# Causal scores on four 64 by 64 tiles of TensorE, with the halves of the keys exchanged in odd pairs of heads

## The chip, the core and the metric

The kernel runs on one core of a Trainium2 chip. A core has five engines with an instruction queue each: TensorE (PE, matrix products; PEld is its loading of weights), VectorE (DVE), ScalarE (ACT), GpSimd (POOL) and SyncE (SP, which here only issues DMAs). The metric is the device time of one execution in microseconds (us). The kernel before took 475.58 us (median of three runs, 474.87 to 476.09).

## What is computed

Two blocks follow each other, all in float32. The first is gated linear attention, for 4 batches, 8 heads, 768 positions and a head size of 48:

```
state = alpha[t][:, None] * state + outer(k[t], v[t])     # 48 x 48 per head
y[t]  = q[t] @ state
```

The heads' outputs are laid side by side to x with 384 columns. The second block is a two-layer perceptron with a residual:

```
xn  = (x - mean) / sqrt(var + 1e-6) * g_ln
out = x + max(xn @ w_ch1, 0) @ w_ch2                      # 384 -> 1536 -> 384
```

## The kernel before, in words

**Chunks.** The 768 positions are cut into 6 chunks of 128, so there are 24 attention blocks (chunk c, batch b), written a to x in the order string: a to d are chunk 0, e to h chunk 1, i to x chunks 2 to 5. Inside a block the recurrence becomes matrix products. The logarithms of alpha are summed along the chunk by a product with a triangle of ones (`lps`, L228); q is multiplied by the exponential of that sum and k by that of its negative (`qk`, L235 and L237); both are transposed per pair of heads (`tps`, L251) and copied to `qkT` (L255, L257). The two heads of a pair lie in rows 0 to 47 and 64 to 111.

**Scores (L264).** For each of four pairs and each of the two heads one matmul makes the full 128 keys by 128 queries, `aps[i][:, p]`. Keys are the stationary operand with 128 columns, queries the moving one with 128 columns, and the contraction runs over 48 rows. Head i goes to the PSUM buffer `aps[i]`. An fp32 matmul shows up in the trace as two passes, each a weight load and a matmul, so a block is 16 passes.

**Mask (L268).** One masked copy per head, `copy_predicated` on DVE, takes the scores with key not after query out of PSUM to `at` in SBUF. `at` was set to zero once, and the masked places are never written, so they stay zero. There are two `at`, used in turn.

**Weighted sum (L281, L286).** `yps` collects the state's part (from chunk 1 on) and the product of `at` with v, per pair, head and half of the queries. ACT copies it to `x` (L290), which lives till the perceptron adds it to its output. `sps` (L297) is the new part of the state, DVE adds it to `st` (L302), POOL multiplies `st` by the chunk's gate (L307). x is then normalized (L311 to L318), transposed (`xps`, L325) and copied to `xT` (L327).

**Perceptron.** Chunk 0 is computed plainly (`hidden`, L337, and `project`, L349). Chunks 1 to 5 use combinations of blocks with fewer products: 30 `hps` steps (L510) and 14 `ops` steps (L404) per chunk, whose sums run on DVE and POOL and partly on ACT.

**Buffers.** PSUM has three buffers with tag `a` (shared by `lps`, `tps` and `aps`), three with tag `m` (`hps`, `ops`) and two with tag `s` (`yps`, `sps`, `xps`). `x` has 9 buffers in SBUF. q, k, v and alpha have one raw buffer per batch and input; v of chunk c + 1 is loaded when the state of chunk c has been updated.

**Order.** Each part is a Python generator that yields between its steps. The string `ORDER` is a list of turns: each letter lets one generator take its next step (a to x the attention blocks, A to L the 12 pieces of weights, M the perceptron, S the combined weights, X and N the combined activations, R the relus). The order of instructions on each engine is that of the turns; semaphores make an engine wait where a result or a buffer isn't ready. A wait on TensorE holds everything behind it on TensorE.

```
    with tc.manual_schedule():
        for turn in ORDER:
            next(turns[turn], None)
```

Of the kernel before, what the change touches and what calls it, by code (L numbers as in the profile page):

```python
# [9 lines left out]
FP32 = mybir.dt.float32  # L10
INT32 = mybir.dt.int32
# [10 lines left out]


ORDER = (
    "ababdaacbaabccaabacdacbaabadcbbbdcdAabbbdaBcCccdabAeddbcbdcffcdfeegacfcbagdhfbde"
    "adbceBeegAdhfBCfdeabdfefcAheiBeafdeagjgbecfebcfcgeegfdefdgcghhihfdcgdegCCigMhMgD"
    "DhMjEMEjFMhiDkhfMgfighFheMFFfMMIMEIhIDMgEjhMGhMgjMhgfMGiHMMGGkMMMMHeiJMkMlHJMigM"
    "IMLJilHljMejKKjiLKeLjMhhfjSigSMhMlSMglSlhgiffMKkMhMhSSSMSSSMXiXkikXSXiimjMXXXSSM"
    "MXkMMSkjMMXkMkMMSMMjMmMMjXkmMSlmiMSMMiMkMMXkMjMMMlMlmRMmMMMokSjlMlMnlMnMljnkMMMR"
    "MjnMMMMSMMmMnMMmnRMMRRMoRSkiMlpklniMkpnjmMMRMmMRpkMRMNMMNmMlMiRkmMMiNMMnloMpRMSM"  # L30
    "njNMMkplMoRMMMkMMNmjNMMlMMNNmonnMljomqMMlqMMlnXMMXMXmXnXXMXqMMMXmmXMMooMMMMpMpMn"
    "MMXMMoMoMMMrMoXMnRqoRmoMpMMrpMMMMMMpMMpRnproMMmMMmqMMMrMMMqqMsMMnMnMpJqrRnqsMorM"
    "tMMMMmqMooRppMpotsRMMtRMtMrMRqMRNMoMNMRNMMrMpRMoNsMqMspqpMoMtMMRMMMNMNMMNMMMoMpn"
    "MpNsrrnMtrpqvrquXrXXrXMquXqXsMXsrMXrMqMMXMXuMMMMrMrMLMsMtXMMstMMMtqMsstMMMMMqvRR"
    "MMvMsuMsMtuMMRMMMrMMuwMMMMRMMMvwMvqMttqMMMruRMMRMMsMMRMMMMRMssRtwtsvutxvMRNsvMNN"
    "tMvNsRtRMMMvMtMMuusMMtMMwuuMrMMwwxNxMxvrtNNMMMNMMMtxsMMMuXMXXXMvMvuuXxXXMXvXuMMM"
    "MwwXwMMxMMxMXMMMMMMuvMMxMMuMMwRxMMMwwRMvMwMMMRxuxwxwwMuxMRxvMwMMMxxMMMMMRMMvMMuM"
    "RMMMvMMMxMMRuMRMMRMMNMMMNRMMNMMvMMNMMMwwMMvwMxxRNwRMMNMNNMMMMwxMMvxMXXXXXXMMMMXX"
    "XMMMMMMMMMXMMMMMMMMXMMMMMRRMMMMMMMMMMMMMRMMRMMMMMMMMMMRRMMMRMMRMMMMMMRMNMMMNRNMM"
    "MMNMMMMMMMRMNRMNMMNMMMMNMMMMMMMM"  # L40
)


# [1 line left out]
def kernel(  # L45
# [8 lines left out]
    w_ch2: bass.AP,  # L54
    out: bass.AP,
):

# [22 lines left out]
    nc = tc.nc  # L82

    B, S, H, D = q.shape
    DM = H * D
    DF = w_ch1.shape[1]
    P = 128
    NCB = S // P
    NP = H // 2
# [6 lines left out]
    cpool = ctx.enter_context(tc.tile_pool(name="const", bufs=1))  # L96
    raw = ctx.enter_context(tc.tile_pool(name="raw", bufs=B))
    stage = ctx.enter_context(tc.tile_pool(name="stage", bufs=STAGED))
    work = ctx.enter_context(tc.tile_pool(name="work", bufs=2))
# [5 lines left out]

    r = np.arange(P)
    upto = (r[None, :] >= r[:, None]).astype(np.float32)
    const_np = np.concatenate([upto, np.eye(P, dtype=np.float32)], 1)

    raws = {}  # L110

    def load(c, b, names="akqv"):
        for n, src in (("a", alpha), ("k", k), ("q", q), ("v", v)):
            if n not in names:
                continue
            t = raw.tile([P, H, D], FP32, name=f"r{n}", tag=f"r{n}",
                         bufs=B)
            nc.sync.dma_start(t, src[b, c * P:(c + 1) * P])
            raws[n, c, b] = t

    consts = cpool.tile([P, 2 * P], FP32, name="consts")
    nc.scalar.dma_start(consts, nc.inline_tensor(const_np, name="consts").ap())
    tri, ident = consts[:, :P], consts[:, P:]
    mask = tri.bitcast(INT32)
    for names in ("a", "kq", "v"):
        for b in range(B):
            load(0, b, names)
# [82 lines left out]
    ats = [cpool.tile([P, 2, NP, P], FP32, name=f"at{i}") for i in range(2)]  # L210
# [6 lines left out]
    x_of, xT_of, hT_of = ({} for _ in range(3))  # L217
# [3 lines left out]
    def attention(c, b):  # L221
# [21 lines left out]
        n = c * B + b + (B if c < 2 else B // 2)  # L243
        if c < 2 or 3 * B <= n < NCB * B:
            load(*divmod(n, B), "akq")
        yield
        qkT = work.tile([R, 2, NP, P], FP32, name="qkT", tag="qkT", bufs=2)
# [11 lines left out]
        at = ats[b % len(ats)]  # L259
        aps = [ps.tile([P, NP, P], FP32, name=f"aps{i}", tag="a", bufs=3) for i in range(2)]  # L260
        for p in range(NP):
            for i in range(2):
                rows = slice(64 * i, 64 * i + D)
                nc.tensor.matmul(aps[i][:, p], qkT[rows, 1, p], qkT[rows, 0, p],  # L264
                                 start=True, stop=True)
        yield
        for i in range(2):
            nc.vector.copy_predicated(out=at[:, i], data=aps[i],  # L268
                                      mask=mask.unsqueeze(1).broadcast_to([P, NP, P]))
        yield  # L270
        if c + 1 < NCB:
            with nc.allow_non_contiguous_dma(reason="one row to columns"):
                nc.sync.dma_start(gate, row.rearrange("o a c -> c (o a)"))
        yield
        vt = raws.pop(("v", c, b))
        yps = ps.tile([P, NP, 2, D], FP32, name="yps", tag="s")
        sides = [slice(64 * s, 64 * s + 64) for s in range(2)]
        for p in range(NP):
            if c > 0:
                for s in sides:  # L280
                    nc.tensor.matmul(yps[s, p].rearrange("p a b -> p (a b)"), qkT[:, 0, p, s],  # L281
                                     sts[b][:R, p].rearrange("p a b -> p (a b)"),
                                     start=True, stop=False)
            for i in range(2):
                for s in sides:
                    nc.tensor.matmul(yps[s, p, i], at[:, i, p, s], vt[:, 2 * p + i],  # L286
                                     start=(c == 0), stop=(c == 0 or i == 1))
        yield
        x_of[c, b] = x = work.tile([P, DM], FP32, name="x", tag="x", bufs=9)
        nc.scalar.copy(out=x, in_=yps.rearrange("p a b d -> p (a b d)"))  # L290
        yield
        if c + 1 < NCB:
# [11 lines left out]
        if c + 1 < NCB:  # L304
            load(c + 1, b, "v")
            st = sts[b].rearrange("p a b d -> p a (b d)")
            nc.gpsimd.tensor_mul(st, st, gate.unsqueeze(2).broadcast_to([P, NP, 2 * D]))  # L307
# [280 lines left out]
    def sums():  # L588
# [4 lines left out]
        yield from combine_weights()  # L593

    turns = {chr(ord("a") + n): attention(n // B, n % B) for n in range(NCB * B)}
    turns |= {chr(ord("A") + i): take_weights(i) for i in range(len(pieces))}
    turns |= {"M": mlp(), "S": sums(), "R": relus(),
# [35 lines left out]
```

## Time and profile before

| what | us |
|---|---|
| median of three runs | 475.58 |
| the profiled execution, first to last instruction | 471.8 |
| TensorE busy | 459.0 |
| DVE busy | 327.1 |
| POOL busy | 203.8 |
| ACT busy | 152.0 |
| masked copies, 48 of 724 ns | 32.2 |

Busy time of TensorE counts any time in which at least one matmul is under way. Matmuls are pipelined, and on different parts of the array several run at once, so the length of a group is read from the start of its first instruction to the start of what follows. In the lists of waits a line says which engine and line waited for which, then the total in us, how often, and the longest.

The same page in 40 slices of 11.8 us shows where TensorE and DVE are busy (in tenths):

```profile
PE   5989999999999999999999999999999999999997
DVE  4899997768456985567768378685656576675742
DMA  8988365203112102030211320120010000000000
```

### The profile page before, as it was taken

Reading aid. Unit: us, or ns where it says so; the run is one execution under the profiler, and the core shown is the slowest. Engines: PE = TensorE matmul, PEld = TensorE weight load, DVE = VectorE, ACT = ScalarE, POOL = GpSimd, SP = SyncE. Lnnn points to the kernel's source line nnn. Section 1 sums busy time; section 2 is a strip of 40 time slices with the busy share of each in tenths; the row PEclk is TensorE's granted clock in tenths of the full one; section 3 lists DMA queues with packets and bytes.
Section 4 is the critical chain, followed back from the end, with each engine's and each line's share of the span. In section 5 each row is a group of like instructions: output and inputs, shape, how many; then the busy total and the mean of one; then the engine's idle time right before and its main releaser. Section 6 shows DMA issues by size and latency. Waiting matters only on the chain.

```text
span 471.8 us, 9234 instructions
## 1 busy us (share of the span) xinstructions
PE 459.0 (97%) x3712; PEld 388.5 (82%) x3712; DVE 327.1 (69%) x571; ACT 152.0 (32%) x325; POOL 203.8 (43%) x203
## 2 busy tenths in 40 slices
PE   5989999999999999999999999999999999999997
PEld 3758654566788899988899998899998899987996
DVE  4899997768456985567768378685656576675742
ACT  5676533421132631114341133351203331123300
POOL 5034010049779873127553116573214281145611
PEclk9999999999999999999999999999999999999999
DMA  8988365203112102030211320120010000000000
GB/s 267 334 234 265 78 192 173 83 23 113 52 36 67 35 18 84 8 114 18 86 35 35 100 71 17 35 85 1 33 36 1 1 1 17 18 33 2 0 35 33
DMA packets 32498, 33.84 MB, mean 72 GB/s; under 512 B 13108, under 2 KB 28596, under 8 KB 32456
## 3 DMA queue, kind: packets, MB, share of 16 engines
q1 hardware_dynamic: 31912, 33.12, 22.8%
q8 instruction: 29, 0.48, 0.4%
q10 hardware_dynamic: 544, 0.13, 0.1%
q14 instruction: 13, 0.11, 0.1%
HBM read 28.49 MB, written 4.76 MB: 70 GB/s over the span
## 4 chain that ended last, share of the span: by engine, by line
PE 90%; DMA 4%; DVE 2%; POOL 2%; ACT 2%; SPq 0%; issue 0%; POOLq 0%; DVEq 0%
PE ops L404 29%; PE hps L510 26%; PE hps L337 7%; PE ops L349 7%; PE aps L264 5%; PE yps L286 4%; PE yps L281 4%; PE tps L251 3%; PE lps L228 2%; PE sps L297 2%; PE xps L325 2%; DMA rk<-in_k_dram 2%; DMA ws<-in_moe_w_ch_dram 1%; DMA ra<-in_alpha_dram 1%; DVE w L163 1%; ACT ws L169 0%
## 5 line engine op out<-in xcount | busy, mean ns | idle before, releaser
L307 POOL TENSOR_TENSOR st<-st,gate 128x384 f32<-128x384 f32 x20 | 20.6, 1034 | 76.7 <-issue 30.6
L510 PE MATMUL hps<-sum,w 128*128 128x256 f32 x200 | 51.7, 381 | 0.0
L404 PE MATMUL ops<-w,hT 128*128 128x192 f32 x240 | 42.5, 327 | 0.0
L404 PE MATMUL ops<-w,sum 128*128 128x192 f32 x240 | 42.4, 326 | 0.0
L404 PE MATMUL ops<-ws,hT 128*128 128x192 f32 x240 | 42.3, 326 | 0.0
L562 ACT ACTIVATE hT<-hT 128x512 f32<-128x512 f32 x60 | 36.6, 632 | 16.5 <-POOL hT L548 6.6
L510 PEld LDWEIGHTS hps<-sum,w 128*128 128x128 f32 x200 | 37.1, 190 | 5.2
L404 PEld LDWEIGHTS ops<-w,hT 128*128 128x128 f32 x240 | 39.3, 190 | 0.7
L404 PEld LDWEIGHTS ops<-w,sum 128*128 128x128 f32 x240 | 39.3, 190 | 0.3
L404 PEld LDWEIGHTS ops<-ws,hT 128*128 128x128 f32 x240 | 39.3, 190 | 0.0
L268 DVE COPY_PREDICATED at<-consts,aps 128x512 f32<-128x512 int32 x48 | 32.2, 724 | 10.2 <-PE aps L264 9.9
L286 PE MATMUL yps<-rv,at 128*64 128x48 f32 x768 | 36.4, 219 | 0.0
L422 POOL TENSOR_TENSOR ob<-u,x 128x192 f32<-128x192 f32 x10 | 6.9, 686 | 67.6 <-issue 42.8
L235 POOL TENSOR_TENSOR qk<-rk,ek 128x384 f32<-128x384 f32 x24 | 26.7, 1113 | 19.5 <-ACT ek L232 19.5
L286 PEld LDWEIGHTS yps<-rv,at 128*64 128x64 f32 x768 | 33.0, 137 | 1.3 <-issue 0.7
L529 POOL TENSOR_TENSOR hT<-hT,u 128x512 f32<-128x512 f32 x10 | 12.8, 1284 | 48.6 <-DVE u L528 48.5
L337 PE MATMUL hps<-xT,w 128*128 128x512 f32 x72 | 32.6, 598 | 0.0
L349 PE MATMUL ops<-w,hT 128*128 128x384 f32 x96 | 32.3, 488 | 0.0
L510 PE MATMUL hps<-xT,w 128*128 128x256 f32 x120 | 31.2, 383 | 0.0
L251 PE MATMUL tps<-consts,qk 128*112 128x128 f32 x192 | 29.2, 281 | 1.5 <-DVE at L268 1.0
L264 PE MATMUL aps<-qkT 48*128 48x128 f32 x384 | 28.6, 285 | 1.5 <-DVE at L268 0.8
L251 PEld LDWEIGHTS tps<-consts,qk 128*112 128x112 f32 x192 | 22.8, 137 | 8.8 <-issue 4.1
(127 smaller groups left out, 956.2 us busy)
## 6 DMA issues: line engine op xcount, KB each, us to landing
ws<-in_moe_w_ch_dram SPq DMA_DIRECT2D x12, 768.0 KB
ra<-in_alpha_dram SPq DMA_DIRECT2D x24, 192.0 KB
rk<-in_k_dram SPq DMA_DIRECT2D x24, 192.0 KB
rq<-in_q_dram SPq DMA_DIRECT2D x24, 192.0 KB
rv<-in_v_dram SPq DMA_DIRECT2D x24, 192.0 KB
out_dram<-ob SPq DMA_DIRECT2D x24, 192.0 KB
row<-eq SPq DMA_DIRECT2D x20, 2.0 KB
gate<-row SPq DMA_DIRECT2D x20, 2.0 KB
```

What stands on the lines that cost most here:

```text
L235: nc.gpsimd.tensor_mul(qk[:, 1, :, :D], raws.pop(("k", c, b)), ek)
L251: nc.tensor.transpose(tps[:, p], qks[b][:, i, p].rearrange("p a b -> p (a b)")[:, :R], ident)
L264: nc.tensor.matmul(aps[i][:, p], qkT[rows, 1, p], qkT[rows, 0, p], start=True, stop=True)
L268: nc.vector.copy_predicated(out=at[:, i], data=aps[i], mask=mask.unsqueeze(1).broadcast_to([P, NP, P]))
L281: nc.tensor.matmul(yps[s, p].rearrange("p a b -> p (a b)"), qkT[:, 0, p, s], sts[b][:R, p].rearrange("p a b -> p (a b)"), start=True, stop ...
L286: nc.tensor.matmul(yps[s, p, i], at[:, i, p, s], vt[:, 2 * p + i], start=(c == 0), stop=(c == 0 or i == 1))
L307: nc.gpsimd.tensor_mul(st, st, gate.unsqueeze(2).broadcast_to([P, NP, 2 * D]))
L337: nc.tensor.matmul(hps, w1[:, f, j * P:(j + 1) * P], xT_of[c][:, f], start=(f == 0), stop=(f == NF - 1))
L349: nc.tensor.matmul(ops_of[b], hT_of[c][:, j, b], w2[:, j], start=(j == 0), stop=(j == NJ - 1))
L404: nc.tensor.matmul(acc, quarters(c, b)[0][n][:, j], win["b"][n][:, j], start=(j == 0), stop=(j == HJ - 1))
L510: nc.tensor.matmul(acc[:, i], w, b, start=True, stop=True)
L562: nc.scalar.activation(out=x, in_=x, func=AFT.Relu)
```

## The change

In chunks 0 and 1 nothing is changed but the order. In chunks 2 to 5:

- A matmul of 128 keys by 128 queries becomes two on 64 columns of the array each: keys of the first half with all 128 queries, and keys of the second half with the 64 queries of the second half. Queries of the first half by keys of the second are not computed (the mask drops them).
- In odd pairs the first half of the keys goes to the output rows 64 to 127 and the second half to rows 0 to 63. In even pairs it is the other way round. Head i still has its rows of the array and its own PSUM buffer.
- The masked copy of a head is cut into three: queries of the second half (all rows, all pairs), then the triangle in even pairs (rows 0 to 63) and in odd pairs (rows 64 to 127). The constants hold a second triangle with its rows rolled by 64.
- The odd pairs need v with its halves of keys exchanged: two more DMAs per block from chunk 2 on load it (`rw`), 64 rows each, two pairs of heads of 384 bytes per row.
- The first block of each `at` in chunk 2 sets its odd pairs to zero again, on POOL.
- `x` has 7 buffers instead of 9.
- The string `ORDER` is another one throughout.

```diff
-    "ababdaacbaabccaabacdacbaabadcbbbdcdAabbbdaBcCccdabAeddbcbdcffcdfeegacfcbagdhfbde"
...
+    "abacbaacabbbaabcabdabbcdabaddcaadcbcbdcbABdbbacaccAdcaacedCeaebdfcecbcfeffhdaged"
...
-    const_np = np.concatenate([upto, np.eye(P, dtype=np.float32)], 1)
+    const_np = np.concatenate(
+        [upto, np.roll(upto, P // 2, 0), np.eye(P, dtype=np.float32)], 1)
...
+            if n == "v" and c > 1:
+                t = raws["w", c, b] = raw.tile([P, NP // 2, 2, D], FP32, name="rw", tag="rw",
+                                               bufs=B)
+                odd = src[b, c * P:(c + 1) * P].rearrange("s (g t i) d -> s g t i d", t=2, i=2)
+                for lo, hi in ((0, P // 2), (P // 2, 0)):
+                    nc.sync.dma_start(t[lo:lo + P // 2], odd[hi:hi + P // 2, :, 1])
...
-                nc.tensor.matmul(aps[i][:, p], qkT[rows, 1, p], qkT[rows, 0, p],
-                                 start=True, stop=True)
-        yield
+                if c < 2:
+                    nc.tensor.matmul(aps[i][:, p], qkT[rows, 1, p], qkT[rows, 0, p],
+                                     start=True, stop=True)
+                    continue
+                for half in range(2):
+                    keys, at_rows = (slice(64 * h, 64 * h + 64) for h in (half, half ^ (p % 2)))
+                    nc.tensor.matmul(aps[i][at_rows, p, 64 * half:], qkT[rows, 1, p, keys],
+                                     qkT[rows, 0, p, 64 * half:], start=True, stop=True)
+        yield
+        if c == 2 and b < len(ats):
+            nc.gpsimd.memset(at.rearrange("p i (g t) q -> p i g t q", t=2)[:, :, :, 1], 0.0)
         for i in range(2):
-            nc.vector.copy_predicated(out=at[:, i], data=aps[i],
-                                      mask=mask.unsqueeze(1).broadcast_to([P, NP, P]))
+            if c < 2:
...
+                continue
+            for rows, t, qs in ((slice(0, P), slice(0, 2), slice(P // 2, P)),
+                                (slice(0, P // 2), slice(0, 1), slice(0, P // 2)),
+                                (slice(P // 2, P), slice(1, 2), slice(0, P // 2))):
+                o, a = (x.rearrange("p (g t) q -> p g t q", t=2)[rows, :, t, qs]
+                        for x in (at[:, i], aps[i]))
+                nc.vector.copy_predicated(
+                    out=o, data=a,
+                    mask=mask[rows, t, qs].unsqueeze(1).broadcast_to(list(o.shape)))
...
+        vs = [vr[:, p // 2] if vr and p % 2 else vt[:, 2 * p:2 * p + 2] for p in range(NP)]
...
-                    nc.tensor.matmul(yps[s, p, i], at[:, i, p, s], vt[:, 2 * p + i],
+                    nc.tensor.matmul(yps[s, p, i], at[:, i, p, s], vs[p][:, i],
...
-        x_of[c, b] = x = work.tile([P, DM], FP32, name="x", tag="x", bufs=9)
+        x_of[c, b] = x = work.tile([P, DM], FP32, name="x", tag="x", bufs=7)
```

More of the change, by code (lines that the diff above doesn't have):

```diff
@@ L24 @@
 ORDER = (
-    "ababdaacbaabccaabacdacbaabadcbbbdcdAabbbdaBcCccdabAeddbcbdcffcdfeegacfcbagdhfbde"
[L26 to L40, printed above, removed]
+    "abacbaacabbbaabcabdabbcdabaddcaadcbcbdcbABdbbacaccAdcaacedCeaebdfcecbcfeffhdaged"
+    "dbhBbheegfdCdfcfebefaafbfebdiAgBhejadegfefceeBdgggcieeigdffcdfcCkggijEdchAhdEDjD"
+    "gMMMgiMMEhhMCMkFMhDDgFFMfigGhMEheGfMMMhMMGMfiFIIHHiMGIjMIMHMhlMeMJMHJeLgkKieMMMJ"
@@ new lines @@
+    "hKLLKglfMMgjMfiMglSMhhMhiSMgjShMkSSSglSjgShSSSSKjiSMghjMkhfMSihflXXSMMSXjjXXjkXj"
+    "iiXMmjiXXMMjMMMXmMMklMSiMllMnMiMMMkMlMmMMmRMXkMMSkMMRkMkMMlSMmMMMknMkMjlMnmRknml"
+    "MMSjMMiMlMkMjliMMmMkRMojMMoMMMjoMMMMRRRnmnMMMmRRMMMNnMMmMnMpMnSMNNMiMiRRMMnMpmlm"
+    "MkpMmNolnkRloMknNnjlMMpooNpMmpNMoMljkoMkMlMlMlMoNXXXXnmMXoXMXXoMmmoMrMXMMMMMMpMM"
+    "pMMMMMMMnMXqpMMMXMRqrMMMqqMMMpMRmqMMmnMopMqpoMMMMrnMrRMnsMrnmrsMMMpMqMRMMMqmMRMq"
+    "RMMMtRMMopRoMrMRMMMsMNRoMNMrnMNMMrRMrsNtMMMqMMpMMnoRMMtptqMMMtNNNMMpnMppNMsMMoMp"
@@ new lines @@
+    "MosppMtoqquXXMXurMXqurXrXrXvqqMXrXMMsMMMssMquMMMvMsMMvMquXMtXstMsMMMMMMtMuMqMtRM"
+    "MMMtrsstRtMquMMuMMrMMMRuMrMRuwMsMMMMMRMqRMqMwMMrMMRvvMrMwRMuMRstvvNMwMNuMMsNMRMM"
+    "vMxvsvMsrsMMRNMMMtMMxMMRMMutNttwxttvNNMMMMxsMvsMtNtMxvurvXJxMXMwXwXMwuXMXXXMxvxX"
+    "XMMwvXMuuMMMMMMMMMMwMMMwMLMwxMxuMMMMMMMuxMxwMMMMMMMuMvMMMMxMvMRMMvMMwRMxvRMMMRMw"
+    "RMMRMRMMMRMRwMMMvRNMNMMNMwMMRvRMMMNMMMxMNNwuMxwxuMNxMwMwxMMxNwMxMMMxXXXMXXMXXMXM"
+    "MMMXMXXMMMMMMMMMMMRMMMMMMMMMMMMMMMRMMMMMMMMMRMMMMMMMMMRMMMRMMRMMMRRRMMMNMMRNNMMR"
@@ L41 @@
+    "NMMMMMMMMMMMMMRNMNMMNMMMMNMMMMMM"
 )
@@ L119, in load @@
             raws[n, c, b] = t
-    consts = cpool.tile([P, 2 * P], FP32, name="consts")
+            if n == "v" and c > 1:
[4 more added lines that the diff above has]
+                    nc.sync.dma_start(t[lo:lo + P // 2], odd[hi:hi + P // 2, :, 1])
+    consts = cpool.tile([P, 3 * P], FP32, name="consts")
     nc.scalar.dma_start(consts, nc.inline_tensor(const_np, name="consts").ap())
-    tri, ident = consts[:, :P], consts[:, P:]
-    mask = tri.bitcast(INT32)
+    tri, ident = consts[:, :P], consts[:, 2 * P:]
+    mask = consts[:, :2 * P].bitcast(INT32).rearrange("p (t q) -> p t q", t=2)
     for names in ("a", "kq", "v"):
@@ L263, in attention @@
                 rows = slice(64 * i, 64 * i + D)
-                nc.tensor.matmul(aps[i][:, p], qkT[rows, 1, p], qkT[rows, 0, p],
-                                 start=True, stop=True)
+                if c < 2:
[6 more added lines that the diff above has]
+                                     qkT[rows, 0, p, 64 * half:], start=True, stop=True)
         yield
+        if c == 2 and b < len(ats):
+            nc.gpsimd.memset(at.rearrange("p i (g t) q -> p i g t q", t=2)[:, :, :, 1], 0.0)
         for i in range(2):
-            nc.vector.copy_predicated(out=at[:, i], data=aps[i],
-                                      mask=mask.unsqueeze(1).broadcast_to([P, NP, P]))
+            if c < 2:
+                nc.vector.copy_predicated(out=at[:, i], data=aps[i],
+                                          mask=mask[:, :1].broadcast_to([P, NP, P]))
+                continue
[7 more added lines that the diff above has]
+                    mask=mask[rows, t, qs].unsqueeze(1).broadcast_to(list(o.shape)))
         yield
@@ L274, in attention @@
         yield
-        vt = raws.pop(("v", c, b))
+        vt, vr = raws.pop(("v", c, b)), raws.pop(("w", c, b), None)
+        vs = [vr[:, p // 2] if vr and p % 2 else vt[:, 2 * p:2 * p + 2] for p in range(NP)]
         yps = ps.tile([P, NP, 2, D], FP32, name="yps", tag="s")
```

## The prediction

> **What bounds the kernel now.** I read the busy shares first, then the chain that ended last, then the waits of TensorE before and after its first large matmul, then the score lines themselves.
>
> ```profile
> span 471.8 us, 9234 instructions
> PE 459.0 (97%) x3712; PEld 388.5 (82%) x3712; DVE 327.1 (69%) x571; ACT 152.0 (32%) x325; POOL 203.8 (43%) x203
> ...
> PE 90%; DMA 4%; DVE 2%; POOL 2%; ACT 2%; SPq 0%; issue 0%; POOLq 0%; DVEq 0%
> PE ops L404 29%; PE hps L510 26%; PE hps L337 7%; PE ops L349 7%; PE aps L264 5%; PE yps L286 4%; PE yps L281 4%; PE tps L251 3%; PE lps L228 2%; PE sps L297 2%; PE xps L325 2%; DMA rk<-in_k_dram 2%; DMA ws<-in_moe_w_ch_dram 1%; DMA ra<-in_alpha_dram 1%; DVE w L163 1%; ACT ws L169 0%
> ...
> L268 DVE COPY_PREDICATED at<-consts,aps 128x512 f32<-128x512 int32 x48 | 32.2, 724 | 10.2 <-PE aps L264 9.9
> ```
>
> TensorE is the chain. Busy TensorE isn't proof, since matmuls overlap, so the waits decide. First the waits of TensorE from 46.5 us to the end, then those before 46.5:
>
> ```profile
> PE hps L510 <- DVE hT L553: 1.0, 1, 1.0
> ```
>
> ```profile
> PE lps L228 <- ACT la L225: 5.4, 3, 4.3
> PE tps L251 <- DVE at L268: 1.0, 2, 0.6
> PE aps L264 <- DVE at L268: 0.8, 1, 0.8
> PE aps L264 <- ACT qkT L255: 0.6, 1, 0.6
> PE tps L251 <- ACT qkT L255: 0.5, 1, 0.5
> ```
>
> After 46.5 us TensorE waits 1.0 us in 422: what a block of matmuls loses in length there, the span loses. The 16 changed score blocks (chunks 2 to 5) all lie there. One of them on the timeline, between two other groups:
>
> ```profile
> 118.50 0.39 PE L286 MATMUL yps<-rv,at 128*64 128x48 f32 x8
> 118.72 0.63 PE L297 MATMUL sps<-rv,qk 128*64 128x48 f32 x16
> 119.28 1.16 PE L264 MATMUL aps<-qkT 48*128 48x128 f32 x16
> 120.37 0.59 PE L349 MATMUL ops<-w,hT 128*128 128x384 f32 x1
> ```
>
> From its start to the next group's is 120.37 - 119.28 = 1.09 us; the chain lists nearly every score block at 1.09 too. The 16 are 8 fp32 matmuls in two passes each. The stretch before the first large matmul (46.4 us) is another regime: by the busy times of that stretch DVE works 37.1 us of it and DMA is at 87%.
>
> **What the Trainium skill says.** "TensorE: Matmul & The Clock Gate", Part 3 (The mechanism): matmuls on different tile positions run concurrently; weight loads overlap matmuls only where the row group differs; matmuls start in strict order. The trace agrees with the first. It disagrees with the rest: in the sps group, whose two tiles share all rows and differ in columns, single starts follow each other every 58.4 ns in the 64-column tile and every 45 ns in the 48-column tile, and the faster overtakes by two passes. So the tiles are queues of their own. The same page, section LDWEIGHTS, gives a load's time as columns / 1.2 ns: 107 for 128, 53 for 64. The trace has one pass per 112 ns per tile in aps (128 columns) and 58 in sps and yps: agrees, plus 5. "TensorEngine Tiling (Array Packing)", Key Properties: 64x64 gives four tiles; changing the mode drains TensorE. The trace shows about 0.1 us between the end of aps' streaming and the next group, and the mode changes as often as before. No 64x64 tile is in this trace.
>
> **The change part by part.**
>
> *Scores.* Before, two tiles (one head of a pair each) run 8 passes each. First to last start is 0.884 us, the first interval 0.214 (a 128-column load in the open), the others 0.112; then the last pass, 0.107, and 0.10 of handover: 1.09. After, four tiles, each with 8 passes: per pair of heads one half of the keys meets all 128 queries (128-wide passes) and the other 64 (64-wide). The exchange in odd pairs gives each tile four wide and four narrow passes; without it one column of tiles would keep eight wide ones and nothing would be gained. Taking 112 ns for a wide pass and 58 for a narrow one (the load rate of 64 columns): an opening load of 0.05 (yps' first interval is 0.134 where 0.08 to 0.10 is its steady one), 4 x 0.112 + 4 x 0.058 = 0.68, handover 0.10: 0.83. Gain 0.26 per block, x16 = 4.2 us. Bounds: issue. 32 passes in 0.68 us are 21 ns each, and the fastest rate in the trace is sps' 1/58.4 + 1/45, 25.4 ns per pass. If that is a limit, 32 x 25.4 = 0.81 takes the place of 0.68: gain 0.13 a block, 2.1 us. On the other side a wide pass can't be under 0.107: 4.5 us. I take 4.2, because pairs of loads and matmuls leave 7 ns apart in the trace, so four tiles can be fed in 28 of 58 ns.
>
> *Masked copies (L268).* Two copies of 512 columns become six: per head 256, 128 and 128 columns (the latter on 64 partitions). Same elements, four more instructions. No smaller copy is in the trace; sums out of PSUM are: 690 ns at 512 columns, 355 at 192, so 1.05 ns per column and about 154 fixed. Hence 456 and 322 ns beside 724, 1.10 us instead of 0.72 per head, 12 us of DVE in all. As back-to-back copies overlap by 0.1 (two take 1.34), the low end is 0.80 instead of 0.62, 5.8 us. DVE goes from 327 to 333-339 us, 71-73%, beside a full TensorE: nothing, except where the weighted sum follows closely. In the new order, two blocks have only one other weighted sum (1.6 us: four pairs of 0.40) between their scores and their own yps, against masked copies that now take 1.7 to 2.2 us; before, two blocks stood as close with copies of 1.34. I put 0.2 us on each: +0.4. Bounds 0 to 1.5. Behind this wait all of TensorE is queued.
>
> *v again.* 32 more loads (two of 48 KB per block, pieces of 384 bytes), 1.6 MB, 13 us of issuing on SP at the 0.38 us of the rv loads. SP and DMA are at leisure there (DMA share by stretches: 0.33 from 46 to 128 us, 0.18 then). They use a buffer freed by the block four earlier, whose yps are past when the load of v is queued: no new wait. Consts grow by 64 KB on ACT's queue beside the first alpha loads: 0.2 us at 275 GB/s, bounds 0 and 0.3; the first lps starts at 4.25 behind an alpha, so I take 0.1.
>
> *Memsets.* Two of 512 columns on POOL, about half of the 0.93 us that the 1024-column ones take, long before the copies that need them: nothing (POOL 43% busy).
>
> *x buffers 9 to 7.* In the new order nine copies of x on ACT wait on POOL's late sums, where one did. ACT is 32% busy, but the relus and the copies that free TensorE's m buffers queue behind such a wait. The copies stand behind the product that frees them; price 0, bounds 0 and 2 us (nine waits of a POOL addition's 0.7, a third of it seen by TensorE).
>
> *The order.* All turns are re-dealt. Up to the last normalization before the first large matmul DVE has the same set of work (six pairs of copies, five state sums, three roundings, two gains, seven q products), so that stretch should end alike: 0, bounds -1.5 and +2. The end has the same products and the same POOL chain before 429.7, where the 1.0 us wait is: 0.
>
> Sum against 471.8 us: -4.2 + 0.4 + 0.1 = -3.7, so 468.1 in the profile. The timed median is 475.58, 3.8 above the span (the profiled run's own time was 473.87); -3.7 from the median is 471.9 us.
>
> **Rivals.**
> - *Issue limits the four tiles*: 0.95 us blocks, gain 2.1 - 0.5 = 1.6, 474.0 us. For it: 21 ns per pass is faster than any in the trace. Against: the 7 ns pairs.
> - *The gain comes back as waits*: DVE's longer copies hold the three shared PSUM buffers, or x's seven buffers bind ACT. At 0.2 us for each of 16 blocks, +3.2 and so 475.1, no change. For it: the closest reuse of an aps buffer in the early chunks is already waited for (1.0 + 0.8 us). Against: from chunk 2 on the new order has 4.8 us or more of matmuls before a buffer of aps is reused.
> - *Slower: tiles in the same rows don't stream together*. Then each row group runs its eight wide and eight narrow passes one after the other, 8 x 0.112 + 8 x 0.058 = 1.36 instead of 0.68: 1.51 us a block, +0.42 x 16 = +6.7, 482 us. It turns from gain to loss when the 32 passes take over 0.94 us, 29 ns per pass. Against: sps runs two such tiles with different moving data freely.
> - *Slower: the start moves.* If the re-dealt turns delay the first large matmul (46.4 us) by over 3.7 us, all behind it moves. TensorE loses most of its idle time there, and DVE is 80% busy. For +6: 478. Against: DVE's equal work.
>
> **How the numbers follow.** Forecast 0.62 (its own range 470.0 to 473.6); issue limit 0.14; waits 0.10; serial tiles 0.06; the start 0.08. 0.3% is 1.4 us, what a measurement can tell here: faster means below 474.15. The forecast is faster but for 0.02 of it, the issue limit for two thirds (0.09), waits for 0.03: 0.72; same 0.13 (0.02 + 0.05 + 0.06); slower 0.15 with 0.01 of the waits. The range runs from 469.2 (wide passes at 0.107, no waits, a start 1.5 earlier) to 476.5, which takes in issue and waits and leaves out most of the 0.14 above and a few hundredths below.
>
> **What would show it.** Blocks of aps from chunk 2 with 32 passes and 0.8 to 0.85 us to the next group; DVE at 333 to 339 us; waits of TensorE after the first large matmul under 2 us, the first at 46 +- 1.5 us. Blocks of 0.95 would show issue; over 1.09, serial tiles; waits of tps, lps or yps on the masked copies, the second rival. I am wrong if the blocks are short and the span isn't.

## The result, and the profile after

The changed kernel takes 482.86 us (median of four runs) beside 475.24 us (the three runs of before and a fourth): 7.6 us slower, ratio 1.0154 (95% interval 1.0133 to 1.0174). I had forecast 471.9 us. The score blocks became as short as forecast; one wait of 8.2 us, and what follows it, outweighs them.

Line numbers differ from those of before: scores are L275 (chunks 0 and 1) and L280 (from chunk 2 on), masked copies L287 and L295, the new memset L284, POOL's sums of weights L491. First the page after: span, busy shares and slices.

```profile
span 481.1 us, 9857 instructions
...
PE 457.8 (95%) x3968; PEld 385.2 (80%) x3968; DVE 339.5 (71%) x635; ACT 151.3 (31%) x325; POOL 202.2 (42%) x205
...
PE   6879999995799999999999999999999999999996
...
POOL 5034010149709884325564224474314462145611
PEclk9999999999799999999999999999999999999999
```

Before, TensorE's row had nothing below 9 between its third slice and its last. Now the tenth and eleventh slices read 5 and 7, and in the eleventh the granted clock reads 7 tenths. Busy time of TensorE went down by 1.2 us while the span grew by 9.3 (the profiled execution of the kernel before was 1.4 us shorter than its median, so the spans lie further apart than the times). So look for idle time. Waits of TensorE from 48.8 us to the end (who waited for whom, total us, times, longest):

```profile
PE tps L261 <- DVE at L295: 8.2, 1, 8.2
PE hps L539 <- DVE hT L582: 0.7, 1, 0.7
PE xps L354 <- DVE xn L347: 0.5, 1, 0.5
```

Only one of them is large. Now the block of scores before it, the first in the new form, on TensorE's timeline:

```profile
104.56 0.67 PE L326 MATMUL sps<-rv,qk 128*64 128x48 f32 x16
105.15 0.90 PE L280 MATMUL aps<-qkT 48*64 48x128 f32 x32
105.98 5.43 PE L378 MATMUL ops<-w,hT 128*128 128x384 f32 x16
...
122.92 1.07 PE L261 MATMUL tps<-consts,qk 128*112 128x128 f32 x4 [8.16 <-DVE at L295]
```

The block takes 105.98 - 105.15 = 0.83 us to the next group; before it was 1.09. Its masked copies start 16 us after its scores. DVE's timeline over that time:

```profile
108.70 0.18 DVE L341 BATCH_NORM_AGGREGATE mv<-stats 128x2 f32<-128x6 f32 x1
121.83 1.92 DVE L295 COPY_PREDICATED at<-consts,aps 128x256 f32<-128x256 int32 x6 [12.95 <-POOL at L284]
```

and POOL's:

```profile
106.20 0.83 POOL L336 TENSOR_TENSOR st<-st,gate 128x384 f32<-128x384 f32 x1 [6.07 <-PE aps L280]
106.99 0.99 POOL L245 TENSOR_TENSOR qk<-rk,ek 128x384 f32<-128x384 f32 x1
107.94 1.11 POOL L491 TENSOR_TENSOR rk<-w 128x384 f32<-128x384 f32 x1
109.02 0.45 POOL L491 TENSOR_TENSOR extra<-w 128x128 f32<-128x128 f32 x1
...
121.28 0.52 POOL L284 MEMSET at<- 128x512 f32 x1
```

Read it from the end. TensorE (transpose of a later block) waits for a PSUM buffer with tag `a` that the masked copies have to empty. The copies wait for the memset of `at`. The memset needs nothing by then, but POOL takes instructions in order: 15 us of products and sums stand ahead of it, and the first of them (the state of block h) had itself waited 6 us. All of DVE's other work stands behind the copies. The sums were there before the change too, without a pause, in the tenth and eleventh slices (106 to 130 us) of POOL's row on the page of before:

```profile
POOL 5034010049779873127553116573214281145611
```

The wait has a tail. Here are five stretches around it, each with its length, the time in which TensorE was busy (and its instructions), and the granted clock (the share of its full clock that TensorE was given; then two columns on DMA):

```profile
112.00:114.70 2.70, 2.70 (x10) 1.00 0.00 0
114.80:118.90 4.10, 0.00 (x0) 1.00 0.00 0
119.00:122.90 3.90, 0.00 (x0) 0.50 0.00 0
122.95:125.75 2.80, 2.80 (x8) 0.50 0.00 0
125.80:127.50 1.70, 1.70 (x6) 1.00 0.00 0
```

The clock was halved during the wait, and the first 2.9 us of work after it ran at half the clock.

### The profile page after: what moved, and what is told of

Same layout as the page of the kernel before. It is cut to its first block, busy times and chain, and to the rows that moved or that the text cites. A ratio compares the mean times of both kernels' runs of the same rounds, so it can differ in the third digit from the quotient of the medians.

```text
span 481.1 us, 9857 instructions
## 1 busy us (share of the span) xinstructions
PE 457.8 (95%) x3968; PEld 385.2 (80%) x3968; DVE 339.5 (71%) x635; ACT 151.3 (31%) x325; POOL 202.2 (42%) x205
## 4 chain that ended last, share of the span: by engine, by line
PE 81%; DVE 9%; POOL 5%; issue 3%; DMA 1%; SPq 0%; DVEq 0%; POOLq 0%
PE ops L433 29%; PE hps L539 24%; PE hps L366 7%; PE yps L315 3%; PE tps L261 3%; PE yps L310 3%; PE ops L378 3%; PE lps L238 2%; PE aps L280 2%; PE xps L354 2%; PE sps L326 1%; DMA rq<-in_q_dram 1%; POOL w L491 1%; DVE qk L247 1%; DVE xn L347 1%
## 5 line engine op out<-in xcount | busy, mean ns | idle before, releaser
L336 POOL TENSOR_TENSOR st<-st,gate 128x384 f32<-128x384 f32 x20 | 18.3, 916 | 75.3 <-DVE st L331 55.1
L295 DVE COPY_PREDICATED at<-consts,aps 64x128 f32<-64x128 int32 (+1 forms) x96 | 29.7, 344 | 15.7 <-POOL at L284 12.9
L433 PEld LDWEIGHTS ops<-w,hT 128*128 128x128 f32 x240 | 39.1, 190 | 0.2
L310 PE MATMUL yps<-st,qkT 112*64 112x96 f32 x320 | 29.9, 257 | 0.0
L378 PEld LDWEIGHTS ops<-w,hT 128*128 128x128 f32 x96 | 18.4, 197 | 12.0 <-issue 0.9
L343 ACT ACTIVATE rstd<-mv,eps 128x1 f32<-128x1 f32 x24 | 7.1, 295 | 65.8 <-DVE mv L341 65.8
```

The source lines that it names most:

```text
L295: nc.vector.copy_predicated(out=o, data=a, mask=mask[rows, t, qs].unsqueeze(1).broadcast_to(list(o.shape)))
L378: nc.tensor.matmul(ops_of[b], hT_of[c][:, j, b], w2[:, j], start=(j == 0), stop=(j == NJ - 1))
L433: nc.tensor.matmul(acc, quarters(c, b)[0][n][:, j], win["b"][n][:, j], start=(j == 0), stop=(j == HJ - 1))
```

## The experiments

Ten versions are set beside the kernel before and the change. Times are medians, each measured beside runs of the kernel before on the same chip (its medians lay between 474.4 and 475.2 us); the ratio is to those runs. "From the first large matmul" is read from the traces: from the start of the first `hps` to the end of the last matmul, which leaves out the start (46.3 to 48.7 us in these profiles).

| version | us | ratio to before (95%) | from the first large matmul, us |
|---|---|---|---|
| before | 475.2 | 1 | 422.1 |
| the change | 482.9 | 1.0154 (1.0133 to 1.0174) | 428.7 |
| memsets early on POOL | 472.0 | 0.9937 (0.9924 to 0.9950) | 418.3 |
| memsets on DVE | 471.2 | 0.9937 (0.9923 to 0.9951) | 418.3 |
| memsets on DVE, copies grouped | 471.6 | 0.9939 (0.9925 to 0.9954) | 417.8 |
| old scores, new order | 473.8 | 0.9983 (0.9975 to 0.9991) | 420.7 |
| the same with the memsets on POOL | 484.3 | 1.0207 (1.0192 to 1.0222) | 430.9 |
| the same (no memset), copies cut in three | 473.7 | 0.9985 (0.9977 to 0.9993) | 420.7 |
| the same, cut on both halves of the rows | 474.4 | 1.0003 (0.9993 to 1.0014) | 421.4 |
| no exchange in odd pairs | 472.9 | 0.9969 (0.9960 to 0.9978) | 419.7 |
| new scores, old order | 473.0 | 0.9967 (0.9955 to 0.9980) | 420.6 |
| its control: before with 8 x and 2 output buffers | 475.3 | 1.0009 (1.0000 to 1.0018) | 422.2 |

**Memsets early on POOL.** Only the place in POOL's queue changes:

```diff
-        if c == 2 and b < len(ats):
-            nc.gpsimd.memset(at.rearrange("p i (g t) q -> p i g t q", t=2)[:, :, :, 1], 0.0)
...
         nc.scalar.copy(out=x, in_=yps.rearrange("p a b d -> p (a b d)"))
+        if c == 1 and b >= B - len(ats):
+            nc.gpsimd.memset(at.rearrange("p i (g t) q -> p i g t q", t=2)[:, :, :, 1], 0.0)
         yield
```

> The changed kernel, with the two memsets of at still on POOL but queued in chunk 1, behind the copies of x of its last two blocks, ahead of the sums that combine the weights. Theory A (the memset stood behind POOL's sums, the masked copies behind the memset, TensorE behind the masked copies): the 8.2 us wait at 114.8 us goes, and with it the slow clock after it (1.6) and the wait of xps (0.5): 482.9 - 10.3 = 472.6 us, 471.5 to 473.8; no wait of TensorE over 1.5 us after 49 us; aps blocks stay at 0.83. Theory B (POOL is late there anyway, since it waits for the state of block h, and TensorE pays at that place in any case): a wait of 3 us or more stays between 105 and 130 us, 476 or more. Theory C (six masked copies per block hold the shared PSUM buffers): waits of tps and lps on the masked copies at several blocks, 476 or more.

Measured: 471.97 us, 10.9 less than the change. The wait is gone; nothing took its place. What TensorE still waits for after its first large matmul:

```profile
PE hps L539 <- DVE hT L582: 0.7, 1, 0.7
PE hps L539 <- DVE hT L580: 0.3, 1, 0.3
PE hps L539 <- DVE u L563: 0.2, 1, 0.2
```

Of the 10.4 us between the two traces from the first large matmul, 8.2 are the wait and 0.5 the wait of xps. The rest, 1.7, goes with the slow clock: eight passes of ops took 3.74 us after the wait and take 2.58 otherwise. (An estimate from the clock alone: 2.9 us at half the clock lose 1.4.) Theories B and C fall for that place.

**Old scores, new order.** The memset goes too, and the weighted sum reads v as it was loaded.

```diff
-                if c < 2:
+                if True:
                     nc.tensor.matmul(aps[i][:, p], qkT[rows, 1, p], qkT[rows, 0, p],
...
-            if c < 2:
+            if True:
                 nc.vector.copy_predicated(out=at[:, i], data=aps[i],
```

> The order of the changed kernel, its seven x buffers and its second loads of v, but scores as two 128-wide row tiles with one masked copy per head in all chunks, and no memset. Theory A: as the memset early version but without the gain of 16 x 0.26 us: 472.6 + 4.2 = 476.8 us, 475.5 to 478; aps blocks 1.09; first large matmul at 48.7 us. If the shorter blocks are given back elsewhere (Theory C), it is no slower than the memset early version: 473 or less.

Measured: 473.77 us, not 476.8. The new order by itself is worth 0.8 us by the ratio (1.4 in the traces), and the short blocks on top of it bring 1.8 us in the medians (2.4 in the traces) instead of 4.2. Adding up the times from one TensorE instruction's start to the next, `aps` has 14.39 us in the early memset version and 18.56 here: the 4.17 us are there. `hps` has 165.3 instead of 164.0, and `ops`, `xps` and `yps` 0.4 more together: 1.8 us are given back in small waits. What causes them is the second question.

**Old scores plus the memsets.** The same, with the two lines of the memset where the change has them.

> As the run with old scores in the new order, plus the two memsets on POOL at the place where the change has them. Theory A: the wait of tps on the masked copies comes back at about 114 us, 7 to 9 us long, with the slow clock after it: 473.8 + 10 to 11 = 484 to 485 us, more than the changed kernel. Rival (the wait needs the four-tile scores or the six copies): under 477.

Measured: 484.28 us, 10.5 more than without the memsets, with old scores and whole copies. Its first wait of TensorE after the first large matmul:

```profile
PE tps L261 <- DVE at L287: 7.6, 1, 7.6
```

and on DVE's timeline the masked copies that it waited for:

```profile
120.96 1.35 DVE L287 COPY_PREDICATED at<-consts,aps 128x512 f32<-128x512 int32 x2 [12.94 <-POOL at L284]
```

So the late memset makes the loss by itself: it needs neither the four tiles nor the six copies.

**Memsets on DVE.** One word of the change: `nc.gpsimd.memset` becomes `nc.vector.memset`.

> The changed kernel with the two memsets on DVE instead of POOL, at the same place in the order. Theory A: no wait on POOL, DVE has two instructions of about 0.5 us more in front of two blocks' copies: 472.0 as with the early memsets, up to 473. If what counts is not POOL's queue but that a memset has to precede the copies there, 476 or more.

Measured: 471.22 us. The same two instructions at the same place in the order, 0.49 us each on DVE, cost nothing that shows. POOL's queue was the cost, not the work.

**New scores, old order**, with the memsets early on POOL as in the first version, and its control, the kernel before with the two changes of buffers alone:

```diff
-ORDER = (... of the change)
+ORDER = (... of the kernel before)
...
-        x_of[c, b] = x = work.tile([P, DM], FP32, name="x", tag="x", bufs=7)
+        x_of[c, b] = x = work.tile([P, DM], FP32, name="x", tag="x", bufs=8)
...
-            ob = work.tile([P, DM], FP32, name="ob", tag="ob", bufs=3)
+            ob = work.tile([P, DM], FP32, name="ob", tag="ob", bufs=2)
```

> The order of the kernel before with the scores, masked copies, second loads of v and constants of the change, memsets early on POOL; 8 x buffers and 2 output buffers instead of 9 and 3, so that it fits. Theory A (the late start is the re-dealt order): first large matmul at 46.3 +- 0.5 us, 4.2 us gained in the blocks, 475.2 - 4.2 + 0.4 = 471.4 us, 470.3 to 473 against its control. Rival (the start is late by the larger constants and the second loads of v): first large matmul at 48 or later, 473.5. Theory C: waits of TensorE on masked copies, 475 or more.

> Control for the old order: the kernel before with 8 x buffers and 2 output buffers. If these are at leisure: 475.2 us within 1. If the two output buffers bind (POOL's first sum then waits for a transfer out), 476 to 479.

Measured: 473.0 beside 475.3 us of the control, 2.3 less: forecast about 3.8. The buffers cost the control nothing. The first large matmul starts at 47.1 us here and at 48.2 in the control, where the kernel before, with the same order, had 46.3; the versions in the new order have 47.3 to 48.7. In the control's trace the granted clock was at half from 18.0 to 24.8 us; in that of the kernel before it wasn't. The start varies that much between profiles of the same order, so I can't lay the change's late start to its order. One wait of `yps` on the masked copies shows here, 0.3 us.

**Copies cut in three, old scores.** The third copy is put on rows 0 to 63, with the plain triangle as its mask, since no pair is exchanged here.

```diff
-            if True:
+            if c < 2:
                 nc.vector.copy_predicated(out=at[:, i], data=aps[i],
...
-                                (slice(P // 2, P), slice(1, 2), slice(0, P // 2))):
+                                (slice(0, P // 2), slice(1, 2), slice(0, P // 2))):
```

> As the run with old scores in the new order (473.8 us, no memset), but the masked copy of a head is cut in three as in the change (256, 128 and 128 columns), scores still 128 wide. Theory A' (of the 4.2 us gained in the blocks some 1.8 are given back because DVE's longer masked copies delay the sums that free TensorE's buffers): 473.8 + 1.2 to 2.2 = 475.0 to 476.0. Rival (they are given back because a faster TensorE runs into DVE and POOL by itself, whatever the copies): 473.8 within 0.5.

Measured: 473.67, as without the cut (473.77), and the same 420.7 us from the first large matmul. Theory A' falls: four more instructions per block cost nothing that shows. But these six copies, all on the lower rows or on all, take 1.52 to 1.55 us; in the change they take 1.87 to 1.94. The difference lies in which rows follow which, as the next two versions show.

**Cut on both halves of the rows, old scores.** The slice and its mask are put back, so the third copy of a head is on rows 64 to 127 as in the change. It leaves out scores of the odd pairs and copies others in their place, so it times the copies and doesn't compute the attention.

> Old scores in the new order, masked copies cut in three on the rows of the change (0 to 63, then 64 to 127), so with its switches of rows but with the slower TensorE. It leaves out the scores of odd pairs' first 64 queries by the first 64 keys and copies others in their place. Theory D: six copies in 1.9 us, waits of hps come up: 473.7 + 0.6 to 1.4 = 474.3 to 475.1. Theory E: 473.7 within 0.4.

Measured: 474.43, 0.8 more; 421.4 instead of 420.7 us in the trace, all of it in `hps` (164.0 to 164.8). The copies of one block, first on the lower rows only, then with this switch, then grouped (next version):

```profile
289.22 1.53 DVE L293 COPY_PREDICATED at<-consts,aps 128x256 f32<-128x256 int32 x6
```

```profile
289.53 1.89 DVE L293 COPY_PREDICATED at<-consts,aps 128x256 f32<-128x256 int32 x6
```

```profile
288.21 1.67 DVE L296 COPY_PREDICATED at<-consts,aps 128x256 f32<-128x256 int32 x6
```

**Grouped copies**, on top of the memsets on DVE:

```diff
-        for i in range(2):
...
+            for rows, t, qs in (... as before ...):
+                for i in range(2):
```

> The version with the memsets on DVE, with the six masked copies of a block in another sequence: both heads' copies on all rows, then both on rows 0 to 63, then both on rows 64 to 127. In the traces a copy that follows one on other rows starts 0.30 to 0.34 us after it where the same copy on the same rows starts after 0.19 to 0.20, and six copies take 1.89 us in the changed order where they take 1.53 all on the lower rows. Theory D (these switches of rows make DVE late for TensorE's buffers; some 1.4 us of waits of hps after 120 us): six copies in 1.6 to 1.7 us, the extra time of hps shrinks from 1.3 us to 0.6 or less, 470.5 to 471.0. Theory E (TensorE is simply early): no change, 471.2 within 0.4.

Measured: 471.63 us. From the first large matmul it is 0.5 us shorter (417.8), and `hps` has 0.45 us less; the timed medians (471.2 and 471.6) don't show it. This profile started 1.3 us later, with the granted clock at half from 31.0 to 34.4 us; the three of its six runs whose mean granted clock was 1.0 took 470.65, 470.7 and 471.4 us, too few to decide. The extra time of `hps` shrank from 1.25 to 0.8 us, where Theory D asked for 0.6 or less. So it holds in part: the switch of rows accounts for 0.5 to 0.75 of the 1.8 us. That the rest comes from a TensorE that is early (Theory E) was not shown; I leave it open.

**No exchange.** All copies are on the lower rows or on all here, v is read as it was loaded, and there is no memset.

```diff
-                    keys, at_rows = (slice(64 * h, 64 * h + 64) for h in (half, half ^ (p % 2)))
+                    keys, at_rows = (slice(64 * h, 64 * h + 64) for h in (half, half))
```

> The changed kernel without the exchange in odd pairs: the first half of the keys always goes to rows 0 to 63, so one column of tiles has eight 128-wide passes and the other eight 64-wide ones; copies as in the change, v as loaded, no memset. If each tile is a queue of its own at 112 ns per wide and 58 per narrow pass: 0.05 + 8 x 0.112 + 0.10 = 1.04 us per block instead of 0.83, time 472.0 + 16 x 0.21 = 475.3. If the four tiles share a limit on the rate of passes, the blocks stay near 0.83.

Measured: blocks of 1.03 us (forecast 1.04), here from 103.86 to 104.89:

```profile
103.86 1.10 PE L280 MATMUL aps<-qkT 48*64 48x128 f32 x32
104.89 0.59 PE L376 MATMUL ops<-w,hT 128*128 128x384 f32 x1
```

The time is 472.86 instead of the 475.3 that I had forecast: 0.9 us less than old scores, 16 blocks by 0.06, where the prediction had nothing without the exchange. It gives next to nothing back (`hps` has 164.1 us); whether because its copies stay on the lower rows or because its TensorE is only 1 us ahead, this version doesn't separate. The exchange is worth the other 0.2 us per block, 3.1 us, of which 1.4 are left in the traces.

## Why the prediction was wrong, by its steps

- **Scores: right.** 0.83 us per block forecast, 0.83 measured, 4.17 us in all. Where the Trainium skill ("TensorE: Matmul & The Clock Gate", Part 3) has matmuls start in strict order, the reading of the trace held instead: tiles are queues of their own, and without the exchange the block took the 1.03 us that this reading gives (1.04). The 32 passes in a block of four tiles start within 0.67 us, one every 22 ns, faster than anything before. Rivals "issue limits" and "serial tiles" are out. What failed is "what a block of matmuls loses in length there, the span loses": of 4.2 us, 2.4 arrived.
- **Memsets: the step that failed.** It says "long before the copies that need them: nothing (POOL 43% busy)". Both halves are wrong. DVE was free for the copies 3 us after the scores, and the memset started 12.4 us after that; and a share of 43% over the span said nothing on the stretch where POOL adds up weights without a pause. The page of before had shown it, in the 9 and 7 of POOL's row given above. The price should have been the time from the end of the scores to the end of the memset and of the first head's copies, 16.9 us (106.0 to 122.9), less the matmuls that TensorE still has until it wants a buffer of tag `a`, 8.8 us: a wait of 8.2. With the slow clock behind it this is +10.4 us in the traces and +10.5 to +11.6 in the medians, where I had 0. The sign of it, a wait of tps on the masked copies, stands in the prediction as that of my second rival, that the gain comes back as waits; but there the copies were to be too long, at +3.2 us over all blocks, and here they were late, once. What that rival describes, small waits all along, was 1.8 us.
- **Masked copies: DVE total right, their price not.** DVE went to 339.5 us (forecast 333 to 339), of which 3.7 are one long normalization (below); with the memsets early it was 337.8. I put 0.4 us on two close weighted sums; no wait of yps on the copies showed in the new order. Instead 0.5 to 0.75 us is lost because copies on different rows don't overlap. The trace of before had a hint of it: the two sums into `st` (L302), on rows 0 to 63 and 64 to 111, took 0.34 and 0.36 us and 0.72 together, where two masked copies on all rows overlap by 0.1.
- **The order and the start: 0 missed a small gain of the order.** The new order is 0.8 us better by the ratio; the start lay at 48.7 us in the profile of the change, outside my 46 +- 1.5, and between 46.3 and 48.7 in all.
- **v again, constants, x's buffers (0, 0.1 and 0): nothing speaks against them.** Without the memset TensorE shows no wait on them, though nine copies of x were to wait on POOL. Only the buffers were tried alone, 8 in the old order.
- **The sum.** In the traces, from the first large matmul to the last: order -1.4, blocks -4.2, given back +1.8, memset with the slow clock +10.4, together +6.6 us (428.7 beside 422.1). The timed difference is 7.6; the last 1.0 is within what the start varies by. Without the memset the traces come to -3.8, close to the -3.7 of the prediction, and that is luck: the order brought 1.4 us that I had at 0, and 1.8 us came back where I had 0.4.

## What to carry to other kernels

Price a small instruction by what stands ahead of it in its engine's queue at that time, not by its length or by the engine's share of the span; then follow who waits for it. A constant that has to be laid down in the middle of a kernel belongs on an engine that is in step with its reader (here DVE: one word of the kernel, 10 to 12 us) or well ahead. And a saving on the bounding engine need not come in full: here 4.2 us in the blocks became 2.4, and 2.9 with the copies grouped; what took the rest was not shown.

## What the runs showed of the hardware that I had not expected

- Masked copies out of PSUM: after one of 128 columns (0.28 to 0.31 us long) the next one starts 0.19 to 0.21 us later if it begins at the same row, and 0.29 to 0.34 us later if it begins at another, so the two don't overlap.
- In the 8 us wait the granted clock fell to 0.50 after 4.2 us of idleness, at 119.0 us, and was back at 1.0 at 125.8, 2.9 us after TensorE had begun again; with old scores and the memsets it fell after 3.8 us and came back after 3.0. The Trainium skill ("TensorE: Matmul & The Clock Gate", Part 1) says that the clock falls to half after an idle window of about 3.4 us and returns after a busy one of that length; the traces agree with the half, and with the lengths to within 0.8 us.
- Right after that wait one normalization on DVE (`xn`, median 0.48 us) took 4.16 us while POOL ran sums back to back (4.88 us with old scores and the memsets). In every trace here each `xn` of over 0.6 us, up to 2.86 us in the kernel before, ran beside POOL for most of its length; but some of 0.47 us did too. That points to POOL; whether POOL held it up was not tried.
